# The last output tile's two column passes, split at column 128 instead of 256

## The chip, the cores and the metric

The kernel runs on one core of a Trainium2 chip. The metric is the device time of one execution in microseconds, as the median of several runs. One further execution was taken with the hardware profiler; its span and its rows are what "the profile" and "the trace" mean here.

## The reference

A linear attention with exponential features, followed by a gated feed-forward block. With 8 batches, 8 heads, 576 positions, 64 columns a head and 128 features:

```
proj = x @ w_phi - max|x @ w_phi|;  phi(x) = [exp(proj), exp(-proj)]
num  = phi(q) @ (phi(k)^T @ v);     den = phi(q) @ sum(phi(k)) + 1e-6
x    = (num / den), heads side by side           # 4608 tokens x 512
out  = (relu(x @ w_gate) * (x @ w_val)) @ w_out  # 512 -> 1536 -> 512
```

The output has 4608 x 512 values in float32, and the change concerns only how the last 128 of its rows are computed from `w_out` and stored.

## The kernel before, in words

The whole program is one list of short words (`ORDER`), written out by hand: every word is a step, and each engine runs its steps in the order of the list. There is no scheduler behind it. A word such as `fp.7.2.1:0` names the step (`do_fp`), its arguments (group 7, tile 2, half 1) and the PSUM bank (0); `@ob1` gives the buffer of a ring that it takes. Waits between engines follow from the tiles and banks that steps read and write.

The feed-forward block works in nine groups of 512 tokens. For each group, 12 blocks of 128 of the 1536 inner columns are computed into `h2` (L1065 and L1086), and then four output tiles of 128 tokens x 512 columns. A normal output tile takes 12 matmuls of 512 columns on TensorE, one for each inner block (`do_fo`, L1126, in three steps of four), is evicted from PSUM by ScalarE (`do_oc`, L1135) or VectorE (`do_oe`, L1138), and is stored as 256 KB on SyncE's (SP's) DMA queue (`do_od`, L1145; L1149 for the ninth, mixed group).

One tile, tile 2 of group 7, which finishes last, is done in two column halves of `HD` = 256 columns. Each half is 12 matmuls (`do_fp`, L1157). Half 1 (columns from `HD` on) is computed first; VectorE evicts it (`do_o2`, L1169) and SP stores it (`do_d2`, L1177). Half 0 (columns up to `HD`) is computed last; ScalarE evicts it (`do_o1`, L1166) and issues its store on its own queue (`do_d1`, L1173). Both halves go into the same output buffer, in separate columns. The end of the list is

```
fo.7.0.1:2 fo.7.0.2:2 fp.7.2.1:0 oc.7.0:2@ob1 od.7.0 od.8.0 fo.7.1.0:4 fo.7.1.1:4 fo.7.3.2:1
fo.7.1.2:4 oe.7.3:1@ob2 fp.7.2.0:6 od.7.3 oe.7.1:4@ob1 o2.7.2:0@ob0 od.7.1 d2.7.2 o1.7.2:6 d1.7.2
```

So on TensorE 16 matmuls of tiles 7.1 and 7.3 stand between the two halves. On VectorE the order is: eviction of 7.3, eviction of 7.1, eviction of half 1. On SP: store of 7.3, store of 7.1, store of half 1. On ScalarE the eviction and the store of half 0 come last. The kernel ends when all stores have landed and the engines have met at a barrier (L1213).

Of the kernel before, what the change touches and what calls it, by code (L numbers as in the profile page):

```python
# [260 lines left out]
def kernel(  # L261
# [11 lines left out]
    nc = tc.nc  # L273
    B, H, S, D = q.shape
    F = w_phi.shape[1]
    NTOK, DM = out.shape
# [19 lines left out]
    def ring(name, n, shape, dtype):  # L296
        tiles = [sb.tile(shape, dtype, name=f"{name}_{i}", tag=f"{name}_{i}") for i in range(n)]
        at = {}

        def of(i):  # L300
            if n == 1:
                return tiles[0]
            if i not in at:
                at[i] = fresh.pop(name)
            return tiles[at[i]]

        return of

    bank = [ps.tile([P, 512], FP32, name=f"bank{i}", tag=f"bank{i}") for i in range(8)]
# [27 lines left out]
    ob_of = ring("ob", 3, [P, DM], FP32)  # L337
# [5 lines left out]
    wo_sb = sb.tile([P, NFC, DM], BF16, name="wo", tag="wo")  # L343
# [713 lines left out]
    def h2_of(g, f):  # L1057
        i = NFC * g + f
        if i not in h2_at:
            h2_at[i] = fresh.pop("hs")  # L1060
        return h2[:, h2_at[i]]
# [88 lines left out]
                out=out[r0 : r0 + SM, :], in_=ob_of(4 * g + t)[SM * bb : SM * (bb + 1)]  # L1150
            )

    HD = DM // 2

    def do_fp(bk, g, t, half):
        for f in range(NFC):
            nc.tensor.matmul(  # L1157
                bank[bk[0]][:, 0:HD],
                lhsT=h2_of(g, f)[:, P * t : P * t + P],
                rhs=wo_sb[:, f, HD * half : HD * (half + 1)],  # L1160
                start=(f == 0),
                stop=(f == NFC - 1),
            )

    def do_o1(bk, g, t):
        nc.scalar.copy(ob_of(4 * g + t)[:, 0:HD], bank[bk[0]][:, 0:HD])  # L1166

    def do_o2(bk, g, t):
        nc.vector.tensor_copy(ob_of(4 * g + t)[:, HD:DM], bank[bk[0]][:, 0:HD])  # L1169

    def do_d1(bk, g, t):
        r0 = S * g + P * t
        nc.scalar.dma_start(out=out[r0 : r0 + P, 0:HD], in_=ob_of(4 * g + t)[:, 0:HD])  # L1173

    def do_d2(bk, g, t):
        r0 = S * g + P * t
        nc.sync.dma_start(out=out[r0 : r0 + P, HD:DM], in_=ob_of(4 * g + t)[:, HD:DM])  # L1177

# [39 lines left out]
```

## Time and profile before

| | us |
|---|---|
| median of 3 runs | 372.36 (372.12 to 373.22) |
| the profiled execution's own time | 371.86 |
| span of its trace | 370.1 |
| TensorE busy | 362.3 (98%) |
| VectorE, ScalarE, GpSimd busy | 289.2, 227.1, 156.5 |

The difference of 1.8 us between the profiled execution's time and its span lies outside the trace. TensorE's granted clock is full in every slice. Rows of the timeline give a start in us from the span's start, a duration, the engine and the source line, then what is written from what. "SPq" and "ACTq" rows are issues of DMAs: the row lasts while the engine issues, and the bytes move and land later.

### The profile page before, as it was taken

What the parts mean: (1) busy time and instruction counts of PE and PEld (TensorE: products, weight loads), DVE (VectorE), ACT (ScalarE), POOL (GpSimd) and SP (SyncE); (2) the same over time, 40 slices, a digit from 0 to 9 for tenths busy, and PEclk for the clock granted to TensorE, in tenths of its full rate; (3) what the DMA queues carried; (4) which work ended last, traced back from release to release, by engine and by line L of the source; (5) the groups of instructions that cost most, each with busy time, mean ns of one, the idle gap of its engine ahead of it and who ended that gap; (6) DMA issues with size and microseconds to landing.
All of it is one profiled execution on the core that took longest, in us unless ns stands there. A gap on an engine that the chain in (4) does not pass through costs nothing.

```text
span 370.1 us, 9178 instructions
## 1 busy us (share of the span) xinstructions
PE 362.3 (98%) x3573; PEld 196.8 (53%) x3624; DVE 289.2 (78%) x674; ACT 227.1 (61%) x550; POOL 156.5 (42%) x161
## 2 busy tenths in 40 slices
PE   8999999999999999999999999999999999999996
PEld 6579865446544655454465444654344644444443
DVE  6999999999989999999888877799665746424441
ACT  4999996988588865977774538856763311211111
POOL 8765985294388049613850524423136013100000
PEclk9999999999999999999999999999999999999999
DMA  9999999909747993593255091263420023101114
GB/s 144 253 197 196 178 186 142 182 16 171 135 108 123 158 130 76 83 173 100 58 102 116 14 144 57 46 113 58 126 69 15 2 73 97 47 0 25 33 28 142
DMA packets 90380, 38.09 MB, mean 103 GB/s; under 512 B 64226, under 2 KB 85602, under 8 KB 90338
## 3 DMA queue, kind: packets, MB, share of 16 engines
q0 software_dynamic: 33504, 15.03, 31.6%
q1 hardware_dynamic: 56690, 22.36, 27.5%
q8 instruction: 28, 0.46, 0.5%
q10 hardware_dynamic: 144, 0.13, 0.1%
q14 instruction: 14, 0.11, 0.1%
HBM read 37.81 MB, written 9.44 MB: 128 GB/s over the span
## 4 chain that ended last, share of the span: by engine, by line
PE 87%; issue 4%; DVE 4%; POOL 2%; ACT 1%; DMA 1%; SPq 0%; POOLq 0%; ACTq 0%
PE bank L1065 43%; PE bank L1126 22%; PE bank L768 4%; PE bank L1094 4%; PE bank L891 4%; PE bank L566 2%; PE bank L828 2%; PE bank L429 2%; POOL xu L934 1%; ACT kp L662 1%; DVE h L851 1%; PE bank L1047 1%; PE bank L1157 1%; DMA xTs<-xu 1%; DVE kT L550 1%
## 5 line engine op out<-in xcount | busy, mean ns | idle before, releaser
L1126 PE MATMUL bank<-wo,h 128*128 128x512 bf16 x401 | 96.2, 379 | 1.1 <-issue 0.2
L662 ACT ACTIVATE kp<-bank 128x384 bf16<-128x384 f32 x192 | 84.4, 518 | 15.1 <-PE bank L566 10.1
L1080 ACT CAST val<-bank 128x512 bf16<-128x512 f32 x81 | 47.2, 595 | 73.7 <-PE bank L1065 65.1
L1086 DVE SCALAR_TENSOR_TENSOR h<-bank,val 128x512 bf16<-128x512 f32 x100 | 66.8, 678 | 28.1 <-PE bank L1065 14.2
L1065 PE MATMUL bank<-xTs,wv 128*128 128x512 bf16 x334 | 85.6, 379 | 0.8
L1065 PE MATMUL bank<-xTs,wg 128*128 128x512 bf16 x340 | 85.3, 379 | 0.6
L934 POOL TENSOR_TENSOR xu<-u,r 128x512 bf16<-128x512 f32 x36 | 37.2, 1041 | 96.0 <-DVE r L930 48.1
L843 ACT ACTIVATE qp<-bank 128x512 bf16<-128x512 f32 x128 | 69.2, 620 | 10.7 <-PE bank L828 9.4
L719 POOL TENSOR_TENSOR vs<-vn,ek 128x780 bf16<-128x780 f32 (+2 forms) x40 | 53.7, 1363 | 24.6 <-ACT ek L679 13.5
L1126 PEld LDWEIGHTS <-h 128*128 128x128 bf16 x420 | 39.1, 98 | 45.8 <-issue 2.4
L1065 PEld LDWEIGHTS <-wg 128*128 128x128 bf16 x400 | 37.4, 98 | 41.3 <-issue 0.7
L1065 PEld LDWEIGHTS <-wv 128*128 128x128 bf16 x400 | 36.9, 98 | 40.4 <-issue 0.7
L670 DVE TENSOR_REDUCE mk<-bank 128x3 f32<-128x384 f32 x96 | 49.6, 540 | 2.4 <-ACT kp L662 1.3
L851 DVE TRANSPOSE_TENSOR_REDUCE maxq<-bank 128x16 f32<-128x512 f32 x56 | 37.4, 692 | 6.1 <-ACT qp L843 3.3
L922 DVE TENSOR_TENSOR u<-bank,t 128x195 f32<-128x195 f32 (+1 forms) x108 | 33.8, 329 | 2.8 <-POOL xu L934 0.6
L912 DVE TENSOR_TENSOR t<-bank,cq 128x195 f32<-128x195 f32 (+1 forms) x96 | 30.1, 324 | 6.8 <-PE bank L891 5.9
L891 PEld LDWEIGHTS <-qp 128*128 128x128 bf16 x512 | 23.1, 98 | 12.6 <-issue 2.0
L891 PE MATMUL bank<-kv,qp 128*128 128x65 bf16 x512 | 26.1, 193 | 0.4 <-ACT kv L779 0.2
L1135 ACT COPY ob<-bank 128x512 f32<-128x512 f32 x19 | 11.3, 596 | 22.2 <-PE bank L1126 22.1
L747 POOL TENSOR_TENSOR vr<-vm,ek 64x520 bf16<-64x520 f32 x14 | 14.8, 1057 | 21.3 <-DMA vm<-in_v_dram 10.6
L1138 DVE COPY ob<-bank 128x512 f32<-128x512 f32 x16 | 11.0, 685 | 16.1 <-PE bank L1126 13.8
L768 PEld LDWEIGHTS <-kp 128*128 128x128 bf16 x640 | 21.6, 97 | 2.8 <-ACT qp L843 0.2
(104 smaller groups left out, 375.6 us busy)
## 6 DMA issues: line engine op xcount, KB each, us to landing
out_dram<-ob SPq DMA_DIRECT2D x31, 256.0 KB, 2.4
vn<-in_v_dram SPq DMA_DIRECT2D x24, 256.0 KB, 4.4
kn<-in_k_dram POOLq DMA_DIRECT2D x7, 512.0 KB, 9.9
qn<-in_q_dram POOLq DMA_DIRECT2D x7, 512.0 KB, 7.8
wv<-in_moe_w_val_dram POOLq DMA_DIRECT2D x3, 512.0 KB, 8.0
wg<-in_moe_w_gate_dram POOLq DMA_DIRECT2D x3, 512.0 KB, 8.0
wo<-in_moe_w_out_dram POOLq DMA_DIRECT2D x3, 512.0 KB, 8.7
out_dram<-ob SPq DMA_DIRECT2D x9, 128.0 KB, 2.3
```

What stands on the lines that cost most here:

```text
L662: nc.scalar.activation(kp_of(3 * b + j)[:, i, s].rearrange("p n f -> p (n f)"), bank[bk[0]][:, 0 : 3 * F], AF.Exp, scale=(1.0, -1.0)[s],)
L670: nc.vector.tensor_reduce(mk_of(3 * b + j)[:, :, i], bank[bk[0]][:, 0 : 3 * F].rearrange("p (n f) -> p n f", f=F), axis=AX.X, op=ALU.max, ...
L719: nc.gpsimd.tensor_tensor(vs_of(3 * b + j)[:, s, 0:n].rearrange("p n i e -> p (n i) e")[:, :, 0:e], src[:, lo:hi].rearrange("p h i e -> p ...
L768: nc.tensor.matmul(out_ps[:, h - lo, s, :], lhsT=lhsT, rhs=rhs, start=(at == 0), stop=(at == 2 * n * (C + 1) - 1),)
L843: nc.scalar.activation(qp_of(4 * b + i)[:, s, 4 * hq : 4 * hq + 4].rearrange("p h m -> p (h m)"), bank[bk[0]], AF.Exp, scale=(1.0, -1.0)[s],)
L851: nc.vector.tensor_reduce((maxq0[:, i] if b == 0 else maxq)[:, :, i, 4 * hq : 4 * hq + 4].rearrange("p t h -> p h t"), bank[bk[0]].rearran ...
L891: nc.tensor.matmul(bank[bk[0]][:, E * n : E * (n + 1)], lhsT=qp_of(4 * b + i)[:, s, h, :], rhs=kv_of(b)[:, h, s, 0:E],)
L934: eng.tensor_tensor(xu_of(n).rearrange("p (h d) -> p h d", d=D), u_of(n)[:, :, 0:D], r_of(n).to_broadcast([P, H, D]), op=ALU.mult,)
L1065: nc.tensor.matmul(bank[bk[0]], lhsT=w[:, dc, P * f : P * f + P], rhs=xT(g)[:, dc, :], start=(dc == 0), stop=(dc == NDC - 1),)
L1080: nc.scalar.copy(val_of(NFC * g + f), bank[bk[0]])
L1086: nc.vector.scalar_tensor_tensor(h2_of(g, f), bank[bk[0]], 0.0, val_of(NFC * g + f), op0=ALU.max, op1=ALU.mult)
L1126: nc.tensor.matmul(bank[bk[0]], lhsT=h2_of(g, f)[:, P * t : P * t + P], rhs=wo_sb[:, f, :], start=(f == 0), stop=(f == NFC - 1),)
```

## The change

`HD`, the column at which the last tile is split, becomes 128. Half 1, still computed first, then has 384 columns, and half 0, still computed last, has 128; `do_fp` takes the columns of its half from a pair of slices, and `do_o2` evicts 384 columns. `do_o1`, `do_d1` and `do_d2` are written with `HD` and follow it. The list of steps stays as it is. Lines behind L1155 move down by one.

```diff
-    HD = DM // 2
+    HD = DM // 4
 
     def do_fp(bk, g, t, half):
+        cols = (slice(0, HD), slice(HD, DM))[half]
         for f in range(NFC):
             nc.tensor.matmul(
-                bank[bk[0]][:, 0:HD],
+                bank[bk[0]][:, 0 : cols.stop - cols.start],
                 lhsT=h2_of(g, f)[:, P * t : P * t + P],
-                rhs=wo_sb[:, f, HD * half : HD * (half + 1)],
+                rhs=wo_sb[:, f, cols],
                 start=(f == 0),
                 stop=(f == NFC - 1),
             )
 ...
     def do_o2(bk, g, t):
-        nc.vector.tensor_copy(ob_of(4 * g + t)[:, HD:DM], bank[bk[0]][:, 0:HD])
+        nc.vector.tensor_copy(ob_of(4 * g + t)[:, HD:DM], bank[bk[0]][:, 0 : DM - HD])
```

## The prediction

> **What bounds the kernel now.** I read the page first, for the whole, and then only the last 15 us, because the edit touches no instruction before them. The page:
>
> ```profile
> span 370.1 us, 9178 instructions
> PE 362.3 (98%) x3573; PEld 196.8 (53%) x3624; DVE 289.2 (78%) x674; ACT 227.1 (61%) x550; POOL 156.5 (42%) x161
> PE 87%; issue 4%; DVE 4%; POOL 2%; ACT 1%; DMA 1%; SPq 0%; POOLq 0%; ACTq 0%
> ```
>
> TensorE carries 87% of the chain that ended last. A change that moves its columns without adding any can gain or lose only where TensorE does not set the time: after its last matmuls. The end of that chain (start, us, what):
>
> ```profile
> 356.50 4.32 PE bank L1126 x20
> 360.81 1.31 PE bank L1157 x12
> 362.12 0.05 issue
> 362.18 3.40 PE bank L1126 x15
> 365.58 1.32 PE bank L1157 x12
> 366.90 0.03 ACTq L1166
> ...
> 366.97 0.37 ACT ob L1166
> ```
>
> The two passes of L1157 are the two 256-column halves of the last tile, and 16 matmuls of two other tiles (L1126) stand between them. The chain goes on through the last pass, its eviction on ScalarE and its store. The timeline of the same stretch (start, us, engine, line) shows what else is late there; the second row of L1145 is from a narrower stretch:
>
> ```profile
> 364.75 0.69 DVE L1138 COPY ob<-bank 128x512 f32<-128x512 f32 x1 [6.53 <-PE bank L1126]
> 365.47 1.26 SPq L1145 DMA_DIRECT2D out_dram<-ob  x2
> 365.67 0.69 DVE L1138 COPY ob<-bank 128x512 f32<-128x512 f32 x1 [0.23 <-PE bank L1126]
> 366.39 0.34 SPq L1145 DMA_DIRECT2D out_dram<-ob  x1
> 366.28 0.41 DVE L1169 COPY ob<-bank 128x256 f32<-128x256 f32 x1
> 366.82 0.38 SPq L1177 DMA_DIRECT2D out_dram<-ob  x1
> 366.97 0.37 ACT L1166 COPY ob<-bank 128x256 f32<-128x256 f32 x1 [5.53 <-PE bank L1157]
> 367.37 0.37 ACTq L1173 DMA_DIRECT2D out_dram<-ob  x1
> ```
>
> Four stores are issued within 2 us: tile 7.3 at 365.47, tile 7.1 at 366.39, the half that was computed first (call it the early part, L1169 and L1177) at 366.82, and the late part (L1166, L1173) at 367.37. The early part's eviction does not run when its matmuls end (362.1): it stands on VectorE behind the eviction of tile 7.1, which waits for the 16 matmuls in between. So the early part is stored only 0.55 us ahead of the late one.
>
> Next the DMA views: issue to landing in the last 15 us, then the GB/s of 367 to 369 us in 40 slices of 0.05 us, then the packets of each queue in 368.1 to 368.3 (two rows) and 368.3 to 368.5 (two rows); q1 is SP's queue, q10 ScalarE's.
>
> ```profile
> out_dram<-ob SPq DMA_DIRECT2D x3, 256.0 KB, 2.0
> out_dram<-ob SPq DMA_DIRECT2D x5, 128.0 KB, 2.3
> out_dram<-ob ACTq DMA_DIRECT2D x1, 128.0 KB, 1.8
> GB/s 123 0 0 0 246 164 492 451 328 410 287 451 205 492 492 328 451 246 308 308 307 328 328 430 369 328 328 328 369 328 348 369 328 205 123 21 0 0 0 0
> q1 hardware_dynamic: 73, 0.07, 101.7%
> q10 hardware_dynamic: 3, 0.00, 4.2%
> q10 hardware_dynamic: 57, 0.06, 83.1%
> q1 hardware_dynamic: 20, 0.01, 15.3%
> ```
>
> From the fifth slice (367.20) to the 35th (368.72) bytes move without a gap: 256 KB of tile 7.1, then 128 KB and 128 KB, 524,288 B in about 1.52 us, 345 GB/s. The first of them moves 0.81 us after its issue (367.20 - 366.39), and the late part's first three packets come just before 368.3, 0.9 us after its issue. So from 367.2 on the end is a full transfer queue, whose start is the issue of tile 7.1's store. After the last byte the late part lands (367.37 + 1.8 = 369.17, 0.45 us later), and the span ends 0.93 us after that. This is the reading on which the forecast rests.
>
> **The change, part by part.** The early part becomes 384 columns wide, the late part 128. In the built program the order of instructions on each engine stays as it was, and each waits for the same things.
>
> *TensorE.* Per matmul, 512 columns take 4.32/20 = 0.216 us and 256 take 1.31/12 = 0.109: proportional to columns. No row has 384 columns with 128-row weights; it lies between these two, and by proportion it is 0.163, so the first pass takes 1.95 instead of 1.31: **+0.64 us** (bounds 0, at the pace of 256, and +1.28, at that of 512; proportion holds to 1% between the rows, so I take 0.64). For 128 columns there is a row:
>
> ```profile
> 31.79 0.83 PE L1094 MATMUL bank<-xTs,wv 128*128 128x128 bf16 x12
> L1094 PE MATMUL bank<-xTs,wv x128: 216/219/230, 28.0 to 41.9; 128*128 128x128 bf16 x128
> L1157 PE MATMUL bank<-wo,h x24: 272/272/273, 360.6 to 366.6; 128*128 128x256 bf16 x24
> ```
>
> (0.83 - 0.219)/11 = 0.056 us each, 0.67 for twelve: the last pass is 0.65 shorter, and TensorE ends where it did, at 366.9. What moves is the work in between: the 16 matmuls of tiles 7.1 and 7.3 start and end 0.64 later.
>
> *VectorE and SP, behind those matmuls.* The evictions of tiles 7.3 and 7.1 go to 365.39 and 366.31, their stores to 366.11 and 367.03. The early part's eviction goes from 366.28 to 366.92 and grows. Rows by form (busy, mean ns):
>
> ```profile
> L1138 DVE COPY ob<-bank 128x512 f32<-128x512 f32 x3 | 2.1, 687 | 6.8 <-PE bank L1126 6.8
> L1169 DVE COPY ob<-bank 128x256 f32<-128x256 f32 x1 | 0.4, 414 | 0.0
> L1135 ACT COPY ob<-bank 128x512 f32<-128x512 f32 x1 | 0.6, 585 | 3.7 <-PE bank L1126 3.7
> L1166 ACT COPY ob<-bank 128x256 f32<-128x256 f32 x1 | 0.4, 372 | 5.5 <-PE bank L1157 5.5
> ```
>
> 384 columns lie between 414 and 687 ns; halfway is 0.55 us. It ends at 367.47, and its store follows 0.13 later as before (366.82 against 366.69): 367.60 instead of 366.82, now 192 KB. SP is free then: it issues tile 7.1's store from 367.03 to 367.37.
>
> *ScalarE.* The late part's eviction starts at 366.95; 128 columns by the slope of 585 and 372 ns take 0.27 us (bounds 0 and 0.37), and its store of 64 KB is issued at 367.25 instead of 367.37. So the two stores change places: the early part is issued last, 0.23 us after the point at which the last store went out before.
>
> *The transfers.* Tile 7.1's bytes start at 367.03 + 0.81 = 367.84. The late part's could start at 367.25 + 0.9 = 368.15 and share the queue with them; the early part's are ready at 368.50, when tile 7.1's 0.76 us of bytes, with the late part's among them, are not yet through. So the queue again has no gap, and the same 512 KB at the same 345 GB/s end at 367.84 + 1.52 = 369.36, 0.64 after 368.72. Landing and end follow unchanged. The shorter eviction and smaller store on ScalarE gain nothing: even if the twelve 128-column matmuls ran at the pace of 256 and lost 0.64, the late part would be issued at 367.89 and be ready at 368.79, while 0.57 us of bytes are still to move.
>
> **Sum:** +0.64 us of queue start, 0 elsewhere: 371.86 + 0.64 = 372.50 for the profiled execution (span 370.7). That execution lies 0.50 below the median of the runs; against the median, 372.36 + 0.64 = **373.0 us**. From 0.41 below to 0.8: a third of the queue's rows now carry 512 B, for which I allow up to 0.15.
>
> A transfer priced by itself would give less. The Trainium skill ("DMA: Bandwidth & Descriptors", the section on the anatomy of one DMA) gives a transfer a constant of about 2 us plus its bytes at 436 GB/s, each by itself. By that the last store lands 0.23 + 0.15 later (65,536 B more), and the sum would be an estimated +0.38 instead of +0.64, which is the first rival below. The trace has 1.8 us for the last store of 128 KB, where that rule makes 2.3. The same page (Bandwidth) puts the limit from HBM at about 358 GB/s for a core; the 345 of the full queue agrees.
>
> **The rivals.**
> *The stores do not queue* (0.12). Then the early part's own path counts: issue 0.23 later and 64 KB more, 0.19 at 345 GB/s: +0.42, 372.78. For it: the late part's first packets came 0.9 us after issue although 256 KB were ahead. Against it: the slices without a gap.
>
> *The late part still ends the kernel* (0.06), if the early part's eviction slips ahead of tile 7.1's. Then it is 0.12 earlier and 64 KB less: -0.31, 372.05. Against it: VectorE's order keeps the eviction behind L1138, and L1138 behind TensorE.
>
> *Slower beyond doubt* (0.10): the mixed rows of 2048, 1536 and 512 B of the last three stores drain worse than even rows do. The GB/s of 355 to 371 us, 0.4 us a slice:
>
> ```profile
> DMA  0000000098910000007998910000794999200000
> GB/s 0 0 0 0 0 0 0 20 205 200 205 26 0 0 0 0 0 0 276 369 236 200 205 26 0 0 0 0 276 364 184 374 338 346 85 0 0 0 0 0
> ```
>
> At 358.2 to 359.4 the engines are as busy (8 to 9 tenths) yet move only 205 GB/s, in stores of 64 rows. At that pace the last 512 KB take 2.56 us instead of 1.52: 0.64 + 1.04 = +1.68, 374.04. It decides below 262 GB/s, where 0.48 more takes the sum past 1.12 us. Against it: rows of 1024 B (the slices from 367.95) still moved at 330 to 340.
>
> **How the numbers follow.** The forecast, that the queue starts 0.64 later, has 0.72. Its own range is +0.41 to +0.79, 372.8 to 373.2. A measurement of this kernel can tell about 0.3% (1.12 us) from no change; the forecast is 0.17%. The three runs lie 1.10 us apart, the highest 0.86 above the median, and a reading 0.48 above the forecast is over 0.3%: I take three in ten of its 0.72 for that, 0.22, with 0.02 from the unqueued case and the 0.10 of the slow drain, 0.34. Faster by over 0.3% needs the case of -0.31 and scatter: 0.03. The rest, 0.63, is within. The range goes from the unqueued case less half the runs' spread, 372.3, up to 373.9, near the slow drain.
>
> **What would show it.** Right: the twelve early matmuls take 1.95 us and the late ones 0.67, TensorE ends within 0.05 of 366.9; tile 7.1's store is issued near 367.0; SP issues the early part at 367.6, after ScalarE's 367.25; bytes move without a gap to 369.4; span 370.7. Wrong: bytes ending before 369.1 (no queue), a last issue on ScalarE (order), or under 262 GB/s after 367.9 (slow drain).

## The result, and the profile after

| | before | after |
|---|---|---|
| median of 22 runs, us | 372.37 (371.77 to 373.28) | 373.00 (372.43 to 373.95) |
| ratio, 95% interval | | 1.0019 (1.0011 to 1.0026) |
| the profiled execution's own time and span | 371.86, 370.1 | 373.07, 371.3 |

The change makes the kernel slower by 0.19%, 0.63 us at the median and 0.66 us between the lowest runs. It is clear of noise over 22 runs, and under the 0.3% that the prediction took as its bound. The forecast was 373.0 and the range 372.3 to 373.9. One run of the kernel before, among those of the experiments below, took 954.69 us and is left out of every ratio.

The page of the changed kernel begins:

```profile
span 371.3 us, 9177 instructions
PE 362.8 (98%) x3573; PEld 196.7 (53%) x3624; DVE 289.5 (78%) x674; ACT 227.1 (61%) x550; POOL 156.4 (42%) x161
```

TensorE has the same number of instructions and, within 0.5 us, the same busy time. The two profiled executions differ by more, 1.2 us. Of these 0.54 us arise in the first 8 us, ahead of anything that the change touches. This is the chain of waits near the start, of the kernel before and of the changed kernel (start, us, what):

```profile
4.44 1.30 PE bank L619 x6
5.74 0.68 PE bank L429 x6
7.48 2.39 ACT kp L662 x6
```

```profile
4.44 1.28 PE bank L619 x6
5.72 1.24 PE bank L429 x6
8.03 2.39 ACT kp L662 x6
```

The same step starts 0.55 us later. All later times of the changed kernel are therefore read from a common event near the end: the start of ScalarE's eviction of tile 7.0, the last one ahead of the edit. From there to the end of the span I call the **tail**. In the timeline of before it starts at

```profile
360.85 0.58 ACT L1135 COPY ob<-bank 128x512 f32<-128x512 f32 x1 [3.73 <-PE bank L1126]
```

and the timeline of the changed kernel (the last store of L1145 from a narrower stretch) goes on from it like this:

```profile
361.39 0.59 ACT L1135 COPY ob<-bank 128x512 f32<-128x512 f32 x1 [3.73 <-PE bank L1126]
365.93 0.69 DVE L1138 COPY ob<-bank 128x512 f32<-128x512 f32 x1 [7.17 <-PE bank L1126]
366.59 0.83 PE L1158 MATMUL bank<-wo,h 128*128 128x128 bf16 x12
366.85 0.69 DVE L1138 COPY ob<-bank 128x512 f32<-128x512 f32 x1 [0.23 <-PE bank L1126]
367.56 0.34 SPq L1145 DMA_DIRECT2D out_dram<-ob  x1
367.45 0.55 DVE L1170 COPY ob<-bank 128x384 f32<-128x384 f32 x1
367.50 0.27 ACT L1167 COPY ob<-bank 128x128 f32<-128x128 f32 x1 [5.53 <-PE bank L1158]
367.80 0.37 ACTq L1174 DMA_DIRECT2D out_dram<-ob  x1
368.03 0.35 SPq L1178 DMA_DIRECT2D out_dram<-ob  x1
```

The page gives the span to 0.1 us only; to 0.01 us the two traces end at 370.08 and 371.29. So the tail is 370.08 - 360.85 = 9.23 us before and 371.29 - 361.39 = 9.90 after, 0.67 more, as the runs have it. (The expectations quoted below were written with rounded spans, such as 9.25 before.) The starts are 361.39 - 360.85 = 0.54 apart; that much is taken off any time after when it is held against before. ScalarE's last eviction still starts where it did (367.50 - 0.54 = 366.96, before 366.97), and its store goes out 0.11 earlier. Tile 7.1's store goes out 0.63 later (367.56 - 0.54 = 367.02, before 366.39), and the early part's store is now the last of all.

The end of the chain of waits of the changed kernel shows the change of hands:

```profile
361.35 1.95 PE bank L1158 x12
363.30 0.05 issue
363.35 3.42 PE bank L1126 x15
366.77 0.04 DVEq L1138
366.80 0.04 issue
366.85 0.06 DVE ob L1138
366.90 0.08 issue
366.99 1.01 DVEq L1214
```

It leaves TensorE after the 16 matmuls of tiles 7.1 and 7.3 and goes on through VectorE up to the barrier (now L1214), at 368.00, where VectorE's eviction of the early part ends. Before, it ran through the last pass and ScalarE's eviction (L1166). Neither end of the chain holds a store or its landing; which store ends last is read from the times from issue to landing. The late part lands at 367.80 + 2.0 = 369.80, the early part at 368.03 + 2.3 = 370.33, some 0.96 us ahead of the end. The transfers at the end (issue to landing; below it GB/s of 368 to 370 us in slices of 0.05 us):

```profile
out_dram<-ob SPq DMA_DIRECT2D x1, 192.0 KB, 2.3
out_dram<-ob ACTq DMA_DIRECT2D x1, 64.0 KB, 2.0
```

```profile
GB/s 246 492 287 164 82 0 0 41 246 287 328 451 328 492 328 369 451 328 492 410 328 246 287 246 246 318 379 369 318 379 399 399 338 369 369 399 307 185 62 0
```

Tile 7.1's bytes start at 368.37, 0.81 after their issue, and there is no empty slice until 369.93, as near as the slices tell. So 512 KB take 1.56 us, 336 GB/s, from a start that is 0.63 later.

### The profile page after: what moved, and what is told of

It reads as the page before. It is cut to its first block, busy times and chain, and to the rows that moved or that the text cites. A ratio compares the mean times of both kernels' runs of the same rounds, so it can differ in the third digit from the quotient of the medians.

```text
span 371.3 us, 9177 instructions
## 1 busy us (share of the span) xinstructions
PE 362.8 (98%) x3573; PEld 196.7 (53%) x3624; DVE 289.5 (78%) x674; ACT 227.1 (61%) x550; POOL 156.4 (42%) x161
## 3 DMA queue, kind: packets, MB, share of 16 engines
HBM read 37.81 MB, written 9.44 MB: 127 GB/s over the span
## 4 chain that ended last, share of the span: by engine, by line
PE 87%; issue 4%; DVE 4%; POOL 2%; ACT 1%; DMA 1%; DVEq 0%; SPq 0%; POOLq 0%
PE bank L1065 43%; PE bank L1126 22%; PE bank L768 4%; PE bank L1094 4%; PE bank L891 4%; PE bank L429 2%; PE bank L566 2%; PE bank L828 2%; POOL xu L934 1%; ACT kp L662 1%; DVE h L851 1%; PE bank L1047 1%; DMA xTs<-xu 1%; DVE kT L550 1%; DVE h L1086 1%
## 5 line engine op out<-in xcount | busy, mean ns | idle before, releaser
L1135 ACT COPY ob<-bank 128x512 f32<-128x512 f32 x19 | 11.3, 595 | 22.1 <-PE bank L1126 22.1
```

## The experiments

The theory is the prediction's: the last stores form a queue without a gap, it starts with tile 7.1's store, and its length is its bytes. The rival is that each store counts by itself, so that the early part's own late issue and larger size make the time. The runs scatter upward by 1 to 2 us from a sharp lowest value, and most differences here are smaller than that, so each kernel is judged by its tail and, beside it, by its lowest run against the lowest run of the kernel before on the same chip.

| kernel | tail, us | lowest run, against before | ratio, 95% interval |
|---|---|---|---|
| before | 9.23 | | |
| changed | 9.90 | +0.66 | 1.0019 (1.0011 to 1.0026) |
| early_out_128 | 9.41 | +0.15 | 1.0004 (0.9993 to 1.0015) |
| early_out_256 | 9.21 | -0.04 | 0.9997 (0.9987 to 1.0008) |
| close_128 | 8.98 | -0.25 | 0.9987 (0.9979 to 0.9996) |
| close_256 | 9.17 | -0.05 | 1.0007 (0.9995 to 1.0019) |
| half_71_128 | 9.59 | +0.35 | 1.0007 (0.9995 to 1.0019) |
| half_71_256 | 9.20 | -0.04 | 1.0001 (0.9992 to 1.0010) |
| late_384 | 9.44 | +0.23 | 1.0000 (0.9991 to 1.0008) |
| close_192 | 9.04 | -0.20 | 0.9990 (0.9977 to 1.0003) |
| close_64 | 9.58 | +0.33 | 1.0003 (0.9992 to 1.0014) |

The lowest runs follow the tails within 0.03 us in every row. The ratios are clear of 1 only for the changed kernel and close_128; for the others the tail and the lowest run alone speak.

**Taking the early part out of the queue.** VectorE idles for over 6 us ahead of tile 7.3's eviction, and the early part has long been computed. Here it is evicted and stored there:

```diff
-fo.7.1.2:4 oe.7.3:1@ob2 fp.7.2.0:6 od.7.3 oe.7.1:4@ob1 o2.7.2:0@ob0 od.7.1 d2.7.2 o1.7.2:6 d1.7.2
+fo.7.1.2:4 o2.7.2:0@ob0 oe.7.3:1@ob2 fp.7.2.0:6 d2.7.2 od.7.3 oe.7.1:4@ob1 od.7.1 o1.7.2:6 d1.7.2
```

With the split at 128:

> The changed kernel (384 columns first, 128 last), but VectorE evicts the 384 columns ahead of tile 7.3's eviction and SP stores them ahead of tile 7.3's store, instead of behind tile 7.1. Matmuls stay as in the changed kernel. The measure is the tail, from the start of ScalarE's eviction of tile 7.0 to the end of the span: 9.25 us before, 9.9 changed. Theory (the full transfer queue that starts with tile 7.1's store sets the end): 192 KB leave that queue, so 0.57 less than the changed kernel at 345 GB/s: tail 9.3 to 9.4, and +0.07 us against the kernel before. Rival (the end follows the early part's own eviction and store, without a queue): the late part or tile 7.1 alone would then be last, bytes end 0.1 to 0.3 ahead of the kernel before: tail 8.9 to 9.15.

With the split at 256:

> The kernel before (256 and 256), with the same move of the early part's eviction and store ahead of tile 7.3's. Theory: tile 7.1's bytes still start near 367.3 of the old trace, 128 KB less are behind them, and the late part, issued as before, then waits for its own start 0.9 us after issue and 0.38 us of bytes: end 0.05 to 0.1 earlier than before, tail 9.15 to 9.2. Rival (no queue, the last store's own path): 0, tail 9.25.

Timeline of early_out_128, and its GB/s of 368 to 370 us:

```profile
364.79 0.56 DVE L1170 COPY ob<-bank 128x384 f32<-128x384 f32 x1 [6.63 <-DMA out_dram<-ob]
365.38 0.34 SPq L1178 DMA_DIRECT2D out_dram<-ob  x1
366.04 1.25 SPq L1145 DMA_DIRECT2D out_dram<-ob  x2
367.20 0.37 ACTq L1174 DMA_DIRECT2D out_dram<-ob  x1
```

```profile
GB/s 369 451 410 369 451 410 369 410 328 256 236 277 266 277 236 72 21 0 0 0 0 0 0 0 0 0 0 0 0 0 0 0 0 0 0 0 0 0 0 0
```

The matmuls, tile 7.1's eviction and its store are as late as in the changed kernel. The 192 KB have left the queue, and the tail falls by 0.49, from 9.90 to 9.41; the rival wanted 8.9 to 9.15. The late part, on ScalarE's own queue and issued as early as in close_128 below, takes 2.0 us to land; there, with tile 7.1 out of the way, it takes 1.7:

```profile
out_dram<-ob ACTq DMA_DIRECT2D x1, 64.0 KB, 2.0
```

So it waits for tile 7.1's bytes though they are on SP's queue. The gain is 0.08 short of the 0.57 expected. Part of that can be read off the changed kernel's row: the slices in which the early part moves alone (369.50 to 369.80) average 379 GB/s, not 345, so its 192 KB were worth about 0.52. With the split at 256 the same move gives 9.21, 0.02 less than before, and 0.04 by the lowest runs. The theory had 0.05 to 0.1 and the rival 0, so this run does not decide between them.

**Both passes at the end.** Now the early pass is moved behind the 16 matmuls, so that tiles 7.1 and 7.3 are stored first:

```diff
-fo.7.0.1:2 fo.7.0.2:2 fp.7.2.1:0 oc.7.0:2@ob1 od.7.0 od.8.0 fo.7.1.0:4 fo.7.1.1:4 fo.7.3.2:1
-fo.7.1.2:4 oe.7.3:1@ob2 fp.7.2.0:6 od.7.3 ...
+fo.7.0.1:2 fo.7.0.2:2 oc.7.0:2@ob1 od.7.0 od.8.0 fo.7.1.0:4 fo.7.1.1:4 fo.7.3.2:1
+fo.7.1.2:4 oe.7.3:1@ob2 fp.7.2.1:0 fp.7.2.0:6 od.7.3 ...
```

> The changed kernel, but the pass of 384 columns is moved behind the 16 matmuls of tiles 7.1 and 7.3, directly ahead of the pass of 128. Theory: tiles 7.1 and 7.3 are now stored 1.3 us earlier than in the kernel before, and are out of the queue at the end; the early part is issued near 366.9 and the late part near 367.26 of the old trace, together 256 KB from 367.75: bytes end near 368.5, 0.23 us ahead of the kernel before and 0.87 ahead of the changed kernel: tail 9.0. Rival (the early part's own eviction and store set the end whatever is queued): it is issued 0.1 later than in the kernel before with 64 KB more: tail 9.4 or more.

> The kernel before, with the first 256-column pass moved behind the 16 matmuls of tiles 7.1 and 7.3. Theory: only the late part's 128 KB are left for the end, on their own path: 0.07 us ahead of the kernel before, tail 9.15 to 9.2. So in this order the split at 128 is worth 0.15 us to the good, where in the old order it costs 0.65. Rival: no difference between the splits' signs in the two orders, that is, the 128 split is again some 0.4 to 0.65 us slower than this kernel.

Timeline of close_128:

```profile
360.79 0.59 ACT L1135 COPY ob<-bank 128x512 f32<-128x512 f32 x1 [3.73 <-PE bank L1126]
364.10 1.25 SPq L1145 DMA_DIRECT2D out_dram<-ob  x2
366.19 0.56 DVE L1170 COPY ob<-bank 128x384 f32<-128x384 f32 x1 [1.20 <-PE bank L1158]
366.78 0.33 SPq L1178 DMA_DIRECT2D out_dram<-ob  x1
366.91 0.27 ACT L1167 COPY ob<-bank 128x128 f32<-128x128 f32 x1 [5.53 <-PE bank L1158]
367.20 0.37 ACTq L1174 DMA_DIRECT2D out_dram<-ob  x1
```

Both 256 KB stores are issued from 364.1 on, and only 256 KB are left for the end. The tail is 8.98 against an expected 9.0; with the split at 256 it is 9.17, within the 9.15 to 9.2 expected. So the same split at 128 costs 0.67 in the old order and gains 0.19 in this one (0.20 between the lowest runs, 371.75 and 371.55). This version beats the kernel before by its interval (0.9979 to 0.9996), which lies wholly below the changed kernel's (1.0011 to 1.0026).

By itself this does not rule out that the early part's own lateness makes the changed kernel's time: here it is issued 5.99 us after the common event, about as before (5.97), and 0.65 earlier than in the changed kernel (6.64). Its landing does. The same store of 192 KB on SP, with nothing ahead of it, takes

```profile
out_dram<-ob SPq DMA_DIRECT2D x1, 192.0 KB, 1.9
```

where it takes 2.3 in the changed kernel, behind tile 7.1. Unqueued, issued at 6.64, it would have landed at 8.54 and the kernel ended 0.93 later: an estimated tail of 9.47, against the 9.90 measured.

**Cutting bytes and nothing else.** Tile 7.1's store leaves out half its columns, whose output stays unwritten:

```diff
+            if g == 7 and t == 1:
+                nc.sync.dma_start(out=dst[:, 0 : DM // 2], in_=ob_of(4 * g + t)[:, 0 : DM // 2])
+                return
             nc.sync.dma_start(out=dst, in_=ob_of(4 * g + t))
```

On the changed kernel:

> The changed kernel, but the store of tile 7.1 leaves out its columns from 256 on (128 KB not written; that half of the tile's output stays empty). Everything is issued at the same times. Theory (full queue from tile 7.1's store on): 128 KB less in the queue, 0.38 us less than the changed kernel, tail 9.5. Rival (no queue; the early part's own store sets the end): 0, tail 9.9. Tail is from the start of ScalarE's eviction of tile 7.0 to the end of the span: 9.25 before, 9.9 changed.

On the kernel before:

> The kernel before with the same half of tile 7.1's store left out. Theory: the queue empties before the late part is ready (0.9 us after its issue), so of the 0.38 us only 0.05 to 0.1 are gained, tail 9.15 to 9.2; the changed kernel has more bytes waiting and gains more from the same cut. Rival (no queue): 0 in both.

Issues of half_71_128 as late as in the changed kernel, and its GB/s of 368 to 370 us:

```profile
367.02 0.34 SPq L1146 DMA_DIRECT2D out_dram<-ob  x1
367.26 0.37 ACTq L1177 DMA_DIRECT2D out_dram<-ob  x1
367.49 0.35 SPq L1181 DMA_DIRECT2D out_dram<-ob  x1
```

```profile
GB/s 348 430 348 348 267 318 297 256 297 349 410 328 348 399 399 399 276 399 399 308 185 62 0 0 0 0 0 0 0 0 0 0 0 0 0 0 0 0 0 0
```

128 KB of another tile, in a store that is not the last, take 0.31 us off the changed kernel's tail (9.59), where the rival had 0. No slice is empty until the last bytes have started. The 0.31 is a little under the 0.38 expected; this cut also shortens tile 7.1's rows from 2048 to 1024 B, but whether that makes the 0.07 was not measured. Off the kernel before the same cut takes only 0.03 (9.20), 0.04 by the lowest runs: there the late part ends on its own path within a few hundredths of the queue. That is under the 0.05 to 0.1 expected and too little to tell from the rival's 0.

**The split the other way.**

```diff
-    HD = DM // 2
+    HD = 3 * DM // 4
```

> The split the other way: 128 columns first, 384 last. Theory: tile 7.1's matmuls end 0.64 earlier than in the kernel before, its bytes and the early part's are gone by 367.6 of the old trace, and the late part stands alone: eviction of 0.48 us instead of 0.37, issue 0.1 later, 192 KB instead of 128: bytes end near 368.9, +0.15 us against the kernel before, tail 9.4. So moving the split costs in both directions, by two different limits. Rival (the sum is symmetric: what 128 costs, 384 gains): -0.64, tail 8.6.

Timeline of late_384:

```profile
361.30 0.58 ACT L1135 COPY ob<-bank 128x512 f32<-128x512 f32 x1 [3.73 <-PE bank L1126]
365.28 1.26 SPq L1145 DMA_DIRECT2D out_dram<-ob  x2
367.42 0.48 ACT L1167 COPY ob<-bank 128x384 f32<-128x384 f32 x1 [5.53 <-PE bank L1158]
367.93 0.37 ACTq L1174 DMA_DIRECT2D out_dram<-ob  x1
```

Counted from the common event, the 256 KB stores go out 0.64 earlier than before (365.28 - 361.30 = 3.98, before 365.47 - 360.85 = 4.62), and it gains nothing: the tail is 9.44, 0.21 more (0.23 by the lowest runs), where 0.15 was expected. What 128 costs, 384 does not give back, since then the late part's eviction and bytes stand alone at the end. In the ratio it is not to be seen.

**How small the late part should be** in the better order: `HD = 3 * DM // 8` and `HD = DM // 8`.

> As the kernel with both passes of the last tile at the end and a split at 128 (tail 9.01 us, 0.23 under the kernel before by its fastest runs), but split at 192. Theory: the early part (320 columns) is issued 0.4 us earlier and out of the way, the late part is issued 0.05 later and its 96 KB come out on their own path, in rows of 768 B: bytes end within 0.03 us of the split at 128, tail 9.0. Rival (the split at 128 still waits for the queue, so fewer columns in the early part gain): tail 8.85 to 8.9, as 32 KB fewer in the early part and its issue 0.4 earlier would give.

> The same order, split at 64: 448 columns, then 64. Theory: the early part's eviction ends near 367.3 of the old trace and its 224 KB, with the late part's 32 KB in rows of 256 B among them, start near 368.1: bytes end at 368.85 to 368.95, tail 9.4 to 9.45, 0.4 more than the split at 128, and the early part is issued last again. Rival (a smaller late part is always better in this order): tail under 9.0.

192 gives nearly the same tail as 128, 9.04 against 8.98, and not the 8.85 to 8.9 of the rival. 64 is worse, 9.58, and by about 0.15 more than expected. Its timeline and its GB/s of 368 to 370 us:

```profile
361.47 0.58 ACT L1135 COPY ob<-bank 128x512 f32<-128x512 f32 x1 [3.73 <-PE bank L1126]
367.82 0.39 ACTq L1174 DMA_DIRECT2D out_dram<-ob  x1
367.84 0.33 SPq L1178 DMA_DIRECT2D out_dram<-ob  x1
```

```profile
GB/s 0 0 0 0 0 0 0 0 0 0 0 0 0 215 179 430 430 230 456 225 461 271 389 420 241 451 246 292 195 78 31 5 0 0 0 0 0 0 0 0
```

The last slice with bytes starts at 369.55, that is at 368.93 of the old trace, within the 368.85 to 368.95 expected. The rest is not in the bytes: the span ends 1.50 us after that slice's start (371.05 - 369.55), where it is 1.33 (370.08 - 368.75) before and 1.39 (371.29 - 369.90) in the changed kernel. The Trainium skill ("DMA: Bandwidth & Descriptors", Specifications) says that transfers of under 512 B are done as read-modify-write. These rows of 256 B are the only rows of output in this study under that size; whether it is this that holds the end back, one kernel does not settle.

## Why the prediction was right

*The reading that the end is a full transfer queue which starts with tile 7.1's store.* Shown for the changed kernel: 192 KB fewer behind that store give 0.49, 128 KB fewer in it 0.31 at the same issue times, and the same 192 KB store lands 0.4 sooner after its issue where nothing is ahead of it. Taking that store out of the end turns the change's loss into a gain, as the reading says, though the rival would allow that too. For the kernel before, the reading is only just true. There the same cuts gain 0.02 to 0.03, and close_256, which leaves nothing but the late part for the end, gains 0.06: the late part's own path ends within a few hundredths of the queue. The prediction saw that no slice was empty, and did not work out how little the queue was ahead. Had the late part ended well after the queue, the change would have cost less than 0.64 by that distance; that the two ends met is luck, and not something the prediction had worked out. The prediction also read the chain of before as going through ScalarE's store; its rows end with the eviction.

*The first pass 0.64 longer, TensorE's end unmoved.* 1.95 us as in the chain above; ScalarE's last eviction starts 0.01 from where it did. Proportion held for 384 columns, for which before had no row.

*Evictions.* 0.55 us forecast and measured for 384 columns on VectorE, 0.27 for 128 on ScalarE.

*The early part's issue*, forecast 367.60 of the old trace, came at 368.03 - 0.54 = 367.49. This step was mis-sized: I carried over the 0.13 us between the eviction's end and the issue, but before that was SP, still busy until 366.73 with tile 7.1's store. After, SP is free and issues 0.03 us behind the eviction. It cost the forecast nothing, since the queue hides it. In the rival without a queue it counts: with the issue 0.12 instead of 0.23 later, and 1.9 us to landing, that rival comes to about 0.24 instead of 0.42.

*The pace of the queue*, 345 GB/s carried over, was 336: 0.04 us more. Of the 0.15 allowed for the short rows that 0.04 came. With a start 0.63 later the sum is 0.67, the difference of the tails. The prediction also found that the 345 agreed with the limit of 358 GB/s that it took from the Trainium skill ("DMA: Bandwidth & Descriptors", Bandwidth). No run shows that limit at work here: the first eight slices of early_out_128, with tile 7.1's bytes alone, average 405.

*The rivals.* The case without a queue gave +0.42 and is ruled out by the same cuts. The one in which the late part still ends the kernel is ruled out by the landings (369.80 for the late part, 370.33 for the early part). The slow drain needed under 262 GB/s; the queue as a whole kept 336, though its mechanism exists on a small scale. The price of a store by itself from the Trainium skill ("DMA: Bandwidth & Descriptors", Anatomy of one DMA) gave +0.38. That section gives its price for transfers issued by GpSimd, one at a time, while these stores are issued by SP and ScalarE and queue. For these stores, where they stand alone, its constant is too large: ScalarE's last store of 128 KB landed in 1.8 us before, and those of close_128 and late_384 (issue to landing) are

```profile
out_dram<-ob ACTq DMA_DIRECT2D x1, 64.0 KB, 1.7
```

```profile
out_dram<-ob ACTq DMA_DIRECT2D x1, 192.0 KB, 1.9
```

that is, by these rounded times, some 1.6 us and a little for the bytes.

*The span*, forecast 370.7, was 371.3 in the one execution profiled, for the 0.54 us at its start; from the common event it is right to 0.03.

## What to carry to other kernels

At the end of a kernel, count the bytes whose stores are issued in the last two microseconds and divide by the pace of the queue: if that fills the time from the first of them to the end, as in the changed kernel here, the earliest of these stores sets the end, and making the last one smaller while its bytes stay in the queue gains nothing. Work out the last store's own path too, from its issue to its landing with nothing ahead: the end is the later of the two, and in the kernel before they were within a few hundredths of a microsecond. Columns that are moved ahead of other tiles' matmuls delay the stores of those tiles, even when TensorE's total stays the same; in the two orders tried here a narrow last piece paid only in the one where the wide remainder comes directly before it and the other tiles are already out, and there a piece of 64 columns was too narrow. Measure effects of 0.2% and less from an event close to the edit: in the eleven traces here the common event, which lies ahead of every edit's effect, starts anywhere from 360.79 to 361.93 us.

## What the runs showed of the hardware that was not expected

Rows of 512 B drained more slowly than longer ones: in early_out_128 the slices fall from 369 to 451 GB/s with rows of 2048 B to 236 to 277 with rows of 512 B; rows of 1024 B, in the kernel before, mostly kept 328 to 369. The DMA engines are busy 8 to 9 tenths of those slow slices, so it is not that they wait. Over a window of 2 us the late part's 64 KB in rows of 512 B (early_out_128) keep the 16 engines busy for 11.3%, its 128 KB in rows of 1024 B (before) for 19.0%, so half the bytes take 0.6 of the time.

A store on ScalarE's queue waited for bytes on SP's: the same 64 KB landed 2.0 us after their issue behind tile 7.1 (early_out_128) and 1.7 us after it where tile 7.1 was out (close_128).

The late part in rows of 256 B was followed by an end of the span 0.1 to 0.2 us later than the others, for which the cause is open.
